# Loading a linear-attention kernel's first chunk in rows of two tokens, and working on it by pairs of batches

## The chip, the cores and the metric

The kernel runs on one core of a Trainium2 chip. The core has five engines with instruction streams of their own: TensorE (PE in the profile, its weight loads PEld), VectorE (DVE), ScalarE (ACT), GpSimd (POOL) and SyncE (SP), which here only issues transfers. Sixteen DMA engines move data. The metric is the device time of one execution in microseconds (us), as a median over runs.

## The reference

Two parts follow each other. The first is a gated linear attention with a state, for 4 batches, 8 heads, 768 tokens and a head width of 48. The second is a sum over four experts, of width 1024, weighted by normalised routing probabilities, for all 3072 tokens.

```python
f = 1.0 / (1.0 + np.exp(-f_logit))
for t in range(S):
    state = f[:, :, t, :, None] * state + np.einsum('bhd,bhe->bhde', k[:, :, t], v[:, :, t])
    y[:, :, t] = np.einsum('bhd,bhde->bhe', q[:, :, t], state)
x = y.transpose(0, 2, 1, 3).reshape(B * S, H * D)      # 3072 x 384
p = domain_probs / (domain_probs.sum(-1, keepdims=True) + 1e-09)
for e in range(E):
    h = np.maximum(x @ w1[e], 0.0)
    out += p[:, e:e + 1] * (h @ w2[e])
```

## The kernel before

The tokens are cut into 6 chunks of 128 (`C`, `T`). For each chunk `c` and batch `b`, attention is computed in its chunked form:

- `load` fetches f, k, q and v. In memory a token of one head is a row of 48 numbers, 192 bytes, and `srcs` puts the token on the partition. Chunk 0 is loaded batch by batch through SP; its v goes through POOL's queue, which casts it to bf16 on the way.
- `gate1` and `gate2` (ScalarE) compute log(1+exp(-f)). `pe_cs` (TensorE) sums it over the tokens of the chunk with the triangular matrix `Ub`, and `exps` (ScalarE) turns the sums into factors.
- `product` multiplies q and k by the factors (VectorE or POOL), `pe_tp` transposes them on TensorE, and an eviction (`ev_tp`) brings them to SBUF as `QK`.
- `pe_at` forms the scores of four head pairs, `ev_at` multiplies them by the causal mask `mask01` (VectorE), and `pe_y` multiplies the scores by v. `pe_xt` transposes the output into `xT`, the input of the experts.
- `pe_kv`, `ev_kv` and `state` bring the running state forward for the next chunk.

The experts then take all four batches of a chunk together as 512 columns: `mm_h` (L374) is the first layer, `relu` (L383, L385) evicts it, `mm_o` (L389) is the second layer and `ev_o` adds it up with the routing weight from `pn`. For chunk 0 alone, the first layer of expert 0 is cut into pieces of 256, 128, 384 and 128 columns, so that it can begin when the first two batches are ready. Attention of chunk `c+1` is spread among the experts of chunk `c`.

The order on each engine is made at build time. Every step is an `Op` with costs, a priority and dependences, and `Plan.run` is a list scheduler that places the steps on five engines ("DMA" is one of them) and hands out buffers from `rooms`. What it decides is the fixed order in which each engine then runs; the engines wait for each other through semaphores. Until the first expert matmul, the gaps that the plan shows on TensorE are filled with dummy matmuls (L644, the tile `busy`).

Transfers are queued by hand, in part. SP issues chunk 0's loads in the order of this line, in which `add_v` puts v on POOL's queue instead:

```python
for i, x in enumerate("f0 k0 q0 f1 k1 q1 f2 f3 k2 q2 v0 k3 q3 v1 v2".split()):
```

The expert weights follow on POOL's queue in eleven pieces (`w 0` to `w 10`, L246): four half pieces for the first layers of experts 0 and 1, two for the second layer of expert 0, then five whole layers. The function `after` makes some transfers wait for others: the first two v loads for k loads, the first f load of chunk 1 for weight piece 6, the last weight piece for chunk 1's k.

Of the kernel before, what the change touches and what calls it, by code (L numbers as in the profile page):

```python
# [25 lines left out]
class Plan:  # L26
# [22 lines left out]
    def take(self, o):  # L49
# [4 lines left out]
        for k in new:  # L54
            self.slot[k] = self.rooms[k[0]].pop(0)
# [47 lines left out]
def kernel(  # L103
# [35 lines left out]
             "vb": 7, "egs": 8, "QK": 4, "AT": 2, "yb": 2, "xT": 2, "h": 2, "o": 6}  # L139
# [7 lines left out]
    make_upper_triangular(nc, U, val=1.0, diag=True)  # L147
    Ub = const.tile([T, T], BF16)
    nc.gpsimd.tensor_copy(out=Ub, in_=U)
    ident = const.tile([T, T], BF16)  # L150
    make_identity(nc, ident)
# [7 lines left out]
    for i in range(rooms["e"]):  # L159
        pads["e", i] = const.tile([T, 2 * NP * P2 + HD], FP32, name=f"e{i}")  # L160
        nc.gpsimd.memset(pads["e", i][:, 0:2 * NP * P2].rearrange("t (r d i) -> t r d i", r=2, i=NP)[:, :, D:P2, :], 0.0)
    mask01 = const.tile([T, NP * T], FP32)
    nc.gpsimd.memset(mask01, 1.0)
    nc.gpsimd.affine_select(
        out=mask01, in_=mask01, compare_op=ALU.is_ge, fill=0.0,
        base=0, channel_multiplier=-1, pattern=[[0, NP], [1, T]],
    )
# [11 lines left out]
    pn = const.tile([T, E, NR], FP32)  # L179
    psm = const.tile([T, 32], FP32, name="psm")[:, 0:NR]  # L180
# [6 lines left out]
    for nm, a in (("f", f_logit), ("q", q), ("k", k), ("v", v)):  # L187
        srcs[nm] = a.rearrange("b h (c t) d -> c t (b h) d", t=T)
    ins = {}
# [7 lines left out]
        "KV": ([T, 512], FP32), "xp": ([T, KD, T], BF16), "hp": ([128, NT], FP32), "op": ([128, 512], FP32), "pp": ([T, E, NR], FP32),  # L197
    }

    def tl(kind, *key):  # L200

        if (kind, key) not in tiles:
            room = kind if kind in rooms else "ps_m" if kind in ("hp", "op", "pp") else "ps_t"
# [27 lines left out]
    def load(c, nm, b, n):  # L231
        if (c, nm) == (0, "v"):
            ins[c, nm, b] = nc.gpsimd.dma_start(out=tl("vb", c, b), in_=srcs[nm][c, :, b * H:(b + n) * H, :])  # L233
            if b < 2:
                after(ins[c, nm, b], ins[v_gate[b]])
            return
# [7 lines left out]
    def load_w(i, e, which, ks, cols):  # L244
        w, r = (w1_sb, w1_r) if which == 1 else (w2_sb, w2_r)
        ins["w", i] = nc.gpsimd.dma_start(out=w[:, e, ks, cols], in_=r[e][:, ks, cols])  # L246
        if i == w_last:
# [5 lines left out]

    def pe_pp():
        for e in range(E):
            nc.tensor.transpose(out=tl("pp")[:, e], in_=praw[:, :, e], identity=ident32)

    def probs():
        nc.vector.tensor_reduce(out=psm, in_=tl("pp").rearrange("p e r -> p r e"), axis=mybir.AxisListType.X, op=ALU.add)
# [419 lines left out]
```

## Time and profile before

| what | value |
|---|---|
| median of 3 runs | 298.34 us (298.16 to 299.37) |
| span of the profiled execution | 296.6 us |
| what lies around the span, by the median | 1.7 us |
| PE busy | 289.0 us, 97% |
| ACT / DVE / POOL busy | 59% / 43% / 36% |
| first expert matmul starts at | 19.75 us |
| dummy matmuls L644 | 34, 10.9 us busy |
| mean traffic of the DMA engines | 123 GB/s |

The profile is one execution, whose own device time is not given apart from its span; a sum that is made against the span is carried over to the median by the 1.7 us between them. A matmul's duration in the profile contains its way through the array, so the price of one in a stream is read from the distance of starts. "PE 97%" says that TensorE is occupied nearly all the time, not that it is at its peak, and the share says nothing of what a change in the head of the kernel is worth: for that the table of windows and the timeline of the first 30 us are read.

### The profile page before, as it was taken

What the parts mean: (1) busy time and instruction counts of PE and PEld (TensorE: products, weight loads), DVE (VectorE), ACT (ScalarE), POOL (GpSimd) and SP (SyncE); (2) the same over time, 40 slices, a digit from 0 to 9 for tenths busy, and PEclk for the clock granted to TensorE, in tenths of its full rate; (3) what the DMA queues carried; (4) which work ended last, traced back from release to release, by engine and by line L of the source; (5) the groups of instructions that cost most, each with busy time, mean ns of one, the idle gap of its engine ahead of it and who ended that gap; (6) DMA issues with size and microseconds to landing.
All of it is one profiled execution on the core that took longest, in us unless ns stands there. A gap on an engine that the chain in (4) does not pass through costs nothing.

```text
span 296.6 us, 5591 instructions
## 1 busy us (share of the span) xinstructions
PE 289.0 (97%) x2172; PEld 170.0 (57%) x2172; DVE 126.1 (43%) x250; ACT 174.3 (59%) x317; POOL 106.1 (36%) x180
## 2 busy tenths in 40 slices
PE   6899999999999999999999999999999999999995
PEld 2476555567777775555555555555555555555553
DVE  6786012785763673045375235243523222101223
ACT  5656656666684667777477575554475544465440
POOL 5786401138767448144449372243220000000000
PEclk9999999999999999999999999999999999999999
DMA  7999999998979999998979932102432100200002
GB/s 157 200 169 206 207 192 210 189 210 167 201 152 166 191 171 185 209 187 164 198 133 218 179 60 35 27 0 67 122 61 30 27 2 27 80 2 0 0 2 106
DMA packets 136462, 36.43 MB, mean 123 GB/s; under 512 B 126812, under 2 KB 135644, under 8 KB 136436
## 3 DMA queue, kind: packets, MB, share of 16 engines
q1 hardware_dynamic: 125188, 29.35, 52.0%
q0 software_dynamic: 11248, 6.72, 16.4%
q8 instruction: 17, 0.28, 0.4%
q14 instruction: 9, 0.07, 0.1%
HBM read 31.51 MB, written 4.72 MB: 122 GB/s over the span
## 4 chain that ended last, share of the span: by engine, by line
PE 78%; DMA 14%; POOL 3%; SPq 2%; issue 1%; ACT 1%; DVE 0%; POOLq 0%
PE ps_m L389 37%; PE ps_m L374 35%; DMA w_sb<-in_moe_w_dram 10%; DMA k<-in_k_dram 4%; SPq L237 2%; POOL w_sb L246 2%; PE ps_t L325 2%; PE ps_t L340 1%; PE ps_t L336 1%; PE ps_t L273 1%; POOL vb L233 1%; PE ps_t L346 1%; ACT e L293 1%; DVE o L396 0%; ACT xT L226 0%
## 5 line engine op out<-in xcount | busy, mean ns | idle before, releaser
L385 ACT ACTIVATE h<-ps_m 128x512 bf16<-128x512 f32 (+2 forms) x188 | 102.4, 548 | 91.9 <-PE ps_m L374 88.9
L374 PE MATMUL ps_m<-xT,w_sb 128*128 128x512 bf16 (+3 forms) x708 | 152.8, 339 | 0.6 <-ACT xT L226 0.6
L389 PE MATMUL ps_m<-w_sb,h 128*128 128x384 bf16 (+1 forms) x776 | 152.6, 324 | 0.1
L389 PEld LDWEIGHTS <-h 128*128 128x128 bf16 x776 | 75.0, 98 | 59.0 <-DMA w_sb<-in_moe_w_dram 0.3
L396 DVE SCALAR_TENSOR_TENSOR o<-ps_m,pn,o 128x384 f32<-128x384 f32 (+1 forms) x73 | 44.5, 612 | 117.3 <-PE ps_m L389 111.1
L374 PEld LDWEIGHTS <-w_sb 128*128 128x128 bf16 x708 | 65.3, 98 | 43.5 <-issue 0.7
L301 POOL TENSOR_TENSOR qk<-q,e 128x384 bf16<-128x384 f32 x18 | 21.4, 1195 | 36.5 <-ACT e L293 34.3
L360 POOL TENSOR_TENSOR Sf<-Sf,egs 48x192 f32<-48x192 f32 x40 | 20.2, 504 | 36.5 <-DVE Sf L353 34.4
L329 DVE TENSOR_TENSOR AT<-ps_t,mask 128x512 bf16<-128x512 f32 x48 | 30.2, 683 | 5.1 <-PE ps_t L325 5.1
L383 DVE TENSOR_SCALAR h<-ps_m 128x256 bf16<-128x256 f32 (+2 forms) x40 | 19.3, 499 | 26.5 <-PE ps_m L374 13.1
L293 ACT ACTIVATE e<-ps_t 128x384 f32<-128x384 f32 x48 | 26.7, 668 | 5.0 <-PE ps_t L273 3.5
L301 POOL TENSOR_TENSOR qk<-k,e 128x384 bf16<-128x384 f32 x20 | 20.2, 1013 | 8.7 <-ACT e L293 5.5
L353 DVE TENSOR_TENSOR Sf<-Sf,ps_t 48x192 f32<-48x192 f32 x40 | 14.0, 350 | 10.3 <-PE ps_t L346 9.4
L246 POOL DMA_DIRECT2D w_sb<-in_moe_w_dram x11 | 8.8, 807 | 18.5 <-DMA k<-in_k_dram 17.2
L361 POOL CAST sb<-Sf 48x192 bf16<-48x192 f32 x40 | 13.6, 340 | 2.6
L398 ACT ACTIVATE o<-ps_m,pn 128x384 f32<-128x384 f32 x22 | 12.8, 582 | 2.5 <-PE ps_m L389 1.5
L644 PE MATMUL ps_m<-busy 128*128 128x512 bf16 x34 | 10.9, 423 | 1.5 <-DVE busy L144 1.5
L265 ACT ACTIVATE ex<-f 128x768 f32<-128x768 f32 (+1 forms) x14 | 10.4, 746 | 1.8 <-DMA f<-in_f_logit_dram 1.8
L298 POOL DMA_DIRECT2D egs<-e x16 | 9.0, 563 | 6.9 <-ACT e L293 6.9
L340 PE MATMUL ps_t<-vb,AT 128*128 128x48 bf16 x192 | 11.4, 184 | 0.0
L269 ACT ACTIVATE gp<-ex 128x768 bf16<-128x768 f32 (+1 forms) x14 | 10.5, 751 | 0.3
L340 PEld LDWEIGHTS <-AT 128*128 128x128 bf16 x192 | 9.9, 97 | 1.1
(54 smaller groups left out, 120.6 us busy)
## 6 DMA issues: line engine op xcount, KB each, us to landing
out_dram<-o SPq DMA_DIRECT2D x23, 192.0 KB, 2.0
w_sb<-in_moe_w_dram POOLq DMA_DIRECT2D x5, 768.0 KB, 18.0
k<-in_k_dram SPq DMA_DIRECT2D x10, 384.0 KB, 5.6
q<-in_q_dram SPq DMA_DIRECT2D x10, 384.0 KB, 5.5
v<-in_v_dram SPq DMA_DIRECT2D x10, 384.0 KB, 5.7
f<-in_f_logit_dram SPq DMA_DIRECT2D x9, 384.0 KB, 4.6
w_sb<-in_moe_w_dram POOLq DMA_DIRECT2D x6, 384.0 KB, 9.0
f<-in_f_logit_dram SPq DMA_DIRECT2D x6, 192.0 KB, 3.8
```

The lines of the kernel that those rows point to most:

```text
L246: ins["w", i] = nc.gpsimd.dma_start(out=w[:, e, ks, cols], in_=r[e][:, ks, cols])
L293: nc.scalar.activation(out=o, in_=i, func=AF.Exp, scale=1.0 if j else -1.0)
L301: engines[eng].tensor_tensor(out=tl("qk", c, b)[:, j, :, 0:D].rearrange("t (i r) d -> t i r d", r=2), in0=tl("qk"[j], c, b // 2)[:, hh(b), ...
L329: nc.vector.tensor_tensor(out=tl("AT", c, b)[:, r].rearrange("s i t -> s (i t)"), in0=tl("A", c, b, r).rearrange("s i t -> s (i t)"), in1= ...
L340: nc.tensor.matmul(out=y[:, h * D:(h + 1) * D], lhsT=AT[:, r, i, :], rhs=vb[:, h, :], start=(c == 0), stop=True, skip_group_check=True)
L353: nc.vector.tensor_tensor(out=Sf[rows, b], in0=Sf[rows, b], in1=KV[rows, :, r, :], op=ALU.add)
L360: nc.gpsimd.tensor_tensor(out=Sf[rows, b], in0=Sf[rows, b], in1=eg, op=ALU.mult)
L374: nc.tensor.matmul(out=hp(c, e, fc, n0, n1, nf)[:, f], lhsT=w1_sb[:, e, kk, (fc + f) * 128:(fc + f + 1) * 128], rhs=tl("xT", c)[:, kk, n0: ...
L383: nc.vector.tensor_relu(out=dst, in_=src)
L385: nc.scalar.activation(out=dst, in_=src, func=AF.Relu)
L389: nc.tensor.matmul(out=tl("op", c, e, nt, part)[:, cols], lhsT=tl("h", c, e, half_of(c, nt * T))[:, fc, nt * T:(nt + 1) * T], rhs=w2_sb[:, ...
L396: nc.vector.scalar_tensor_tensor(out=o, in0=op, scalar=pe, in1=o, op0=ALU.mult, op1=ALU.add)
```

## The change

Two neighbouring tokens of one head lie side by side in memory. Chunk 0 is now read in rows of two tokens, 384 bytes, which fall on one partition. Since that leaves 64 rows for a batch, two batches share a tile of 128 partitions, alternating (`(p b)`). A unit of work is no longer one batch with 8 heads, but a pair of batches with 4 heads, both token parities `j` side by side: again 128 partitions and 384 columns.

What follows from this:

- Loads of chunk 0 move half as many rows of twice the length, in the order f0 f1 k0 k1 q0 q1 v0 v1 f2 f3 k2 k3 q2 q3, and v2 and v3 after weight piece 0. v0 waits for f1, and weight piece 1 waits for k3.
- The sums over tokens are made with two triangular matrices (`Ui` with the diagonal, `Us` without), which also keep the batches apart; four matmuls of 192 columns take the place of one of 384. The scores of a unit are 16 matmuls on 48 rows and 64 columns of the array instead of 8 on 48 rows and 128 columns. `pe_y0` has 16 matmuls on 64 rows for 8 on 128, and `pe_kv0` 32 in all for 16.
- k is copied within SBUF (`dma_kc`, eight transfers on SP's queue) into `kc`, where the batches lie in separate halves of the partitions. The eviction of the transposes (`ev_tp`) does the same sorting for q and k.
- New constants are made on VectorE at the start: `par`, `parb`, `Ui`, `Us`, `mask0`, and `mask01`, which POOL made before.
- The output tokens of chunk 0 come out sorted by parity. The routing weights are therefore transposed twice (`p_by_j`, `pe_pp`: eight transposes for four), and `store` writes chunk 0 with two transfers per tile.
- The first layers of experts 0 and 1 are computed for the first pair of batches, then for the second pair, in pieces of 256 columns. Experts 2 and 3 are as before.
- `rooms["vb"]` goes from 7 to 4. The first scores and outputs (`A0`, `y0`) take banks of `ps_m` instead of `ps_t`.

The diff, cut to its core:

```diff
-            self.slot[k] = self.rooms[k[0]].pop(0)
+            free = self.rooms[k[0]]
+            self.slot[k] = free.pop(free.index(min(free)) if k[1] in ("A0", "y0") else 0)
...
+    par = const.tile([T, 32], FP32, name="par")[:, 0:2]
+    parb = const.tile([T, 32], BF16, name="parb")[:, 0:2]
+    nc.vector.tensor_reduce(out=par, in_=ident.rearrange("t (p b) -> t b p", b=2), axis=mybir.AxisListType.X, op=ALU.add)
+    nc.vector.tensor_copy(out=parb, in_=par)
+    Ui = const.tile([T, T], BF16, name="Ui")
+    for b in range(2):
+        nc.vector.tensor_single_scalar(out=Ui.rearrange("t (p b) -> t b p", b=2)[:, b], in_=U.rearrange("t (p b) -> t b p", b=2)[:, b],
+                                       scalar=par[:, b:b + 1], op=ALU.mult)
+    Us = const.tile([T, T], BF16, name="Us")
+    nc.vector.tensor_tensor(out=Us, in0=Ui, in1=ident, op=ALU.subtract)
+    mask0 = const.tile([T, 4, P2], FP32, name="mask0")
+    for b in range(2):
+        rows = slice(b * P2, (b + 1) * P2)
+        nc.vector.tensor_copy(out=mask0[rows], in_=U[rows, rows].unsqueeze(1).broadcast_to([P2, 4, P2]))
+        nc.vector.tensor_tensor(out=mask0[rows, 2], in0=mask0[rows, 2], in1=ident[rows, rows], op=ALU.subtract)
...
-    nc.gpsimd.memset(mask01, 1.0)
...
+    nc.vector.tensor_copy(out=mask01.rearrange("s (i t) -> s i t", i=NP), in_=U.unsqueeze(1).broadcast_to([T, NP, T]))
...
+        srcs[nm, 0] = a.rearrange("b h (c p j) d -> c b p h (j d)", p=P2, j=2)[0]
...
+        if c == 0:
+            t = tl(nm, c, b // 2)[:].rearrange("(p b) (h j) d -> b p h (j d)", b=2, j=2)
+            ins[c, nm, b] = nc.sync.dma_start(out=t[b % 2], in_=srcs[nm, 0][b])
+            return
...
+        if i in w_hold:
+            after(ins["w", i], ins[w_hold[i]])
...
+        for j in range(2):
+            for jj in range(2):
+                nc.tensor.matmul(out=cs[:, j * HD // 2:(j + 1) * HD // 2], lhsT=Us if jj > j else Ui, rhs=g[:, jj * NP:(jj + 1) * NP, 0:D],
+                                 start=(jj == 0), stop=(jj == 1))
...
+    def ev_tp(c, b, js, eng):
+        o, i = tl("QK", c, b)[0:MP, js], tl("tp", c, b)[0:MP, js]
+        if c == 0:
+            o, i = o.rearrange("m q i (b p) -> m (q i) b p", b=2), i.rearrange("m q i (p b) -> m (q i) b p", b=2)
+        copy(eng, o, i)
...
+    def dma_kc(n):
+        k = tl("qk", 0, n)[:, 1].rearrange("(p b) h d -> b p (h d)", b=2)
+        for b in range(2):
+            nc.sync.dma_start(out=kc[n // 2][b * P2:(b + 1) * P2, n % 2].rearrange("p h d -> p (h d)"), in_=k[b])
...
+    def pe_at0(n):
...
+                        rows, tok = slice(r * P2, r * P2 + D), slice(b * P2, (b + 1) * P2)
+                        nc.tensor.matmul(out=a_of(0, n, r)[tok, 2 * i + j, :].rearrange("s (k t) -> s k t", k=2),
+                                         lhsT=QK[rows, 1, 2 * j + i, tok], rhs=Q[rows, i, :, tok], start=True, stop=True)
...
+    def pe_y0(n):
...
+                        nc.tensor.matmul(out=y_of(2 * g + b)[:, h * D:(h + 1) * D], lhsT=AT[tok, r, 2 * i + j, :], rhs=v0[g][tok, h, j, :],
+                                         start=(j == 0), stop=(j == 1), skip_group_check=True)
...
-    v_gate, issued = [(0, "k", 1), (0, "k", 2)], []
+    v_gate, w_hold, issued = {0: (0, "f", 1)}, {1: (0, "k", 3)}, []
...
-    for i, x in enumerate("f0 k0 q0 f1 k1 q1 f2 f3 k2 q2 v0 k3 q3 v1 v2".split()):
+    for i, x in enumerate("f0 f1 k0 k1 q0 q1 v0 v1 f2 f3 k2 k3 q2 q3".split()):
...
-            for fcs, n0, n1, xs, nf in ((range(0, KF // 2), 0, N2, LO, 1), (range(0, KF // 2, 2), N2, NT - T, [2], 2),
-                                        (range(KF // 2, KF), 0, NT - T, LO + [2], 1), (range(0, KF, 4), NT - T, NT, [3], 4)):
-                zip_units([(c, 0, fc, n0, n1, xs, nf) for fc in fcs], [])
-            unit[0] = u0 + 2 * KF
+            for e, n0, xs in ((0, 0, LO), (1, 0, LO), (0, N2, HI)):
+                zip_units([(c, e, fc, n0, n0 + N2, xs) for fc in range(KF)], [], 0.5)
+            zip_units([(c, 1, fc, N2, NT, HI) for fc in range(KF)], ol(c, 0, ALL))
+            unit[0] = u0 + 3 * KF
```

A new planner function `attention0` takes the place of `attention` for chunk 0. It adds, for each unit n (0 and 1 for batches 0 and 1, 2 and 3 for batches 2 and 3), gates, sums, factors, products, transposes, scores, masks and y in this order of priority, with the priorities of the second pair behind those of the first; k comes ahead of q, and each is transposed and evicted by itself. Products of units 0 and 1 are for VectorE alone, of units 2 and 3 for VectorE or POOL.

## The prediction

> **What bounds the kernel now.** The page first. TensorE is busy almost throughout, and the DMA engines are saturated for the first fifth only:
>
> ```profile
> PE 289.0 (97%) x2172; PEld 170.0 (57%) x2172; DVE 126.1 (43%) x250; ACT 174.3 (59%) x317; POOL 106.1 (36%) x180
> PE   6899999999999999999999999999999999999995
> DMA  7999999998979999998979932102432100200002
> ```
>
> A table of windows then says where TensorE's idle time lies (columns: stretch, length, busy of PE, weight loads, DVE, ACT, POOL, clock, DMA share, GB/s):
>
> ```profile
> 0.00:19.50 19.50, 16.01 (x151) 8.15 (x152) 13.98 (x34) 11.95 (x27) 14.41 (x29) 1.00 1.22 171
> 19.50:24.00 4.50, 4.50 (x51) 3.55 (x50) 3.26 (x11) 3.35 (x10) 2.49 (x3) 1.00 1.25 206
> 24.00:28.20 4.20, 4.20 (x53) 3.02 (x51) 3.58 (x11) 2.68 (x5) 2.52 (x6) 1.00 1.30 205
> 28.20:59.20 31.00, 30.89 (x186) 16.84 (x184) 8.90 (x15) 19.10 (x34) 6.28 (x13) 1.00 1.18 200
> ```
>
> Before 19.5 most of PE's 16 us are the dummy matmuls (34 of them, 10.9 us). From 19.75, the first expert matmul, PE has no hole to speak of. So the end is the time of that matmul (call it D), plus all PE work still left at D, plus stalls. The timeline of PE around it:
>
> ```profile
> 19.75 0.82 PE L374 MATMUL ps_m<-xT,w_sb 128*128 128x256 bf16 x6
> 20.41 0.33 PE L365 MATMUL ps_t<-ident,yb 128*128 128x128 bf16 x3
> 20.57 0.82 PE L374 MATMUL ps_m<-xT,w_sb 128*128 128x256 bf16 x6
> 21.23 0.36 PE L340 MATMUL ps_t<-vb,AT 128*128 128x48 bf16 x8
> ...
> 22.59 0.33 PE L365 MATMUL ps_t<-ident,yb 128*128 128x128 bf16 x3
> ...
> 24.22 0.84 PE L346 MATMUL ps_t<-vb,qk 128*128 128x96 bf16 x16
> 24.90 3.44 PE L374 MATMUL ps_m<-xT,w_sb 128*128 128x128 bf16 x33
> ```
>
> Starts, not durations, give the price, because a duration holds about 0.16 of pipeline. Six 256-column matmuls take 20.41-19.75 = 0.66, 0.11 each. The x33 group (24 of 128 columns, 9 of 512) lasts from 24.90 to 28.18: at 0.216 for 512 columns the short ones cost 0.055 each. All shapes stream at one rate per column, so regrouping the first expert layers earns nothing by itself. Of chunk 0's attention only 0.16+0.20+0.17+0.68 = 1.2 us lies after D; the rest ran where PE was idle.
>
> The chain of waits up to 60 us is transfers:
>
> ```profile
> 20.53 21.10 DMA w_sb<-in_moe_w_dram
> 42.07 7.75 DMA k<-in_k_dram
> 50.37 8.82 DMA w_sb<-in_moe_w_dram
> 59.24 0.82 PE ps_m L389 x4
> ```
>
> The last weights land at 59.19 and are used at 59.24: PE and DMA are in step. A change must bring both forward.
>
> **What the Trainium skill says.** "DMA: Bandwidth & Descriptors", section "Why small descriptors are slow (HBM only)", gives about 3 cycles per packet beside 32-byte beats; "How a descriptor splits into AXI transactions" says a read starts at a 256-byte boundary, lost bytes paid. Rows of 192 bytes at steps of 192 then cost 6, 12, 10 and 8 beats, mean 9, plus 3: 12 cycles. Rows of 384 cost 12 and 16, mean 14, plus 3: 17. The trace agrees on the first: from the issue-to-landing times, first-chunk loads land about 0.95 us apart (f1 6.24, k2 11.05, five loads between), 64 rows per engine, 14.7 ns a row, against 14.1 at the page's 850 MHz fabric clock. A 384-byte load is not in the trace. Estimate: 0.94 x (512 x 17)/(1024 x 12) = 0.66. Bounds 0.50 (half the rows at the old price) and 0.94 (bytes decide). "TensorEngine Tiling (Array Packing)", section "Key Properties", says tiles run in parallel but changing the mode drains the array. This trace shows eight 48-row products in 0.33 us (60.64 to 60.97), i.e. two side by side, and shows no four-quadrant use.
>
> **Loads.** Sixteen first-chunk loads save 0.28 each: 4.5 us. Added: eight SBUF copies of k, 64 rows of 1 KB each. No such copy is in the trace; by bytes at the 210 GB/s of the early windows 0.3 each, 2.5 in all, and 1.2 at twice that rate; they sit on SP's queue behind the f load of chunk 1, hence after weight piece 6. KV sums wait for them, but are needed only by y of chunk 1 (61 us), 25 us later: no cost there. Weight pieces 1 to 5, now landing at 22.0, 24.1, 26.0, 28.0, 29.9, come 4.5 earlier; the last at 59.2-4.5+(1.2 to 2.5) = about 56.5. Piece 1 gets a new wait, on the last k. Behind it on POOL stand only weight issues (seven took 5.51 us), states, and products that VectorE can take; before it 12.4 us of transfers are queued, so the DMA engines don't run dry.
>
> **When D comes.** A unit is now two batches by half the heads, the same 384 columns; two units finish the first pair. First bytes at 2.0 as now; f1 at 2.0+1.32+0.57 (f0's excess) = 3.9, against f0 alone at 3.5. ScalarE: both units' gates, 4 x 0.52, to 6.15; exps 0.43 each, first k product possible at 6.7. VectorE is not free: its setup ended at 5.45 and gains ten small constant operations. None is in the trace; by like rows (0.10 for a cast, 0.18 for a tensor-scalar, 0.25 for a reduce) 1.8, bounds 1.2 and 2.5: 7.2. Then its line is the path: four products x 0.56, one eviction 0.4, four mask products x 0.64 = 5.2, plus 0.5 for the one place where it waits on TensorE: 12.9. The end of the chain: y 0.5, its copy 0.55, transposes 0.34, copy 0.48, hops and weight load 0.6: D = 15.4. Credit 19.75-15.4 = 4.35. v, gated on f1, lands near 9 to 10 (now 12.8 and 15.65) and isn't late; q3 lands near 15.
>
> **PE work left at D.** The second pair (units 2, 3) now runs inside the dense part. Their cumulative sums and k transposes fit before D (k3 lands near 12.4). After D: q transposes 8 x 0.055 = 0.44; scores 16 per unit, 0.33 (four at once) to 0.66 (two), take 0.5: 1.0; y 16 per unit at 0.025: 0.8; output transposes 0.33; KV 32 instead of 16 half-height matmuls, 0.68 to 1.36, take 1.0; routing transposes, now eight and behind the first pair, 0.127 each: 1.0. Sum 4.6, minus the 1.2 of now: debit 3.4 (bounds 2.3 and 4.5).
>
> **Stalls.** Weights: piece 1 at 17.5; four units of 0.33 and the routing bring PE there at 17.7. Piece 3 at 21.5 against 22.5. Narrow, but enough. The second pair: VectorE's products 2.24, masks 2.56, copies about 1.5 end near 20, its output tiles near 22; PE's first-pair work for two experts (5.3) plus what is mixed in reaches 23.7. 16 relus at 0.39 on ScalarE alone fill 6.2 of those 8. PE's order is fixed, so an attention instruction whose eviction is late holds the expert matmuls behind it: I put 0.6, bounds 0 and 3. The doubled stores of chunk 0 (four more SP issues at about 0.4) the copy that sorts the routing weights by parity (24 rows of 512, at most 0.6 by the 512-column mask product), and fewer v buffers (4 for 7) lie beside work with slack: nothing.
>
> **Sum.** 296.6 - 4.35 + 3.4 + 0.6 = 296.25. The median of the runs is 1.7 above that profile's span; 298.34 - 0.35 = **298.0**, no change. About 0.5% (1.5 us) is what can be told from none: 296.8 to 299.8. The earlier start is real, but bought with attention work that was free in the idle head and now isn't.
>
> **Rivals.** *Cheap quadrants*: scores, y and KV overlap fully (debit 2.3), setup is 1.2, D = 14.8 (credit 4.95), no stall: 295.7. For it: before D PE is slack, and 48-row pairs overlap already. Against: VectorE's 5.2 us line. Chance 0.24.
> *In-order stalls* (slower): attention of the second pair is chained VectorE to PE at ten hand-overs; late by 0.35 each, PE loses about 3: 298.34-0.95+3 = 300.4. It decides once the hand-overs fall behind by more than 0.25 on average, since ten of those eat the 0.95 and 1.5 besides. For it: POOL is issuing weights and VectorE must take all products. Against: ScalarE and VectorE kept up between 19.5 and 28.2 now, where PE had no hole, though with three hand-overs only. Chance 0.24.
> *The rows don't get cheaper* (0.94 per load): weight piece 3 stays at 26.0, PE holds at expert 1's second half; then 1.3+5.2 of expert work and 1.0 of KV end at 33.5, where now 31.4 stands for the same work: 300.4. For it: the DMA engines are full already. Against: the row price fits the page. Chance 0.08.
> The forecast: 0.44, its own range 296.9 to 299.5. Over all cases 295.7 to 300.9. Faster 0.24, same 0.44, slower 0.32.
>
> **What would show it.** Right: first expert matmul near 15.4; first-chunk loads landing 0.6 to 0.7 apart; PE without holes from 15.4 to 28 but with score, y and KV groups between expert matmuls; last weights near 56.5. Wrong: D before 14.5, PE idle of over 1.5 us between D and 30 with VectorE or weights as releaser, or 0.9 per load.

## Result, and the profile after

The changed kernel takes 306.52 us (median of 4 runs, 305.5 to 307.14) against 298.28 for the kernel before beside it: ratio 1.026, 95% interval 1.022 to 1.030. Forecast were 298.0 us and no change, with a range to 300.9. The profiled execution has a span of 304.6 us, 8.0 more than before, with 1.8 around it (before: 1.7).

The page of the changed kernel, the lines that answer to those of before, and the granted clock:

```profile
PE 294.1 (97%) x2265; PEld 176.4 (58%) x2265; DVE 137.4 (45%) x275; ACT 170.7 (56%) x316; POOL 104.4 (34%) x178
PE   5969999999999999999999999999999999999995
PEclk9975999999999999999999999999999999999999
DMA  6999999992899987999796943001432100100002
```

TensorE is again full from the fourth slice on (a slice is 7.6 us), and it is emptier in the first and third than before. Its granted clock falls in the third and fourth. Windows of the same run (stretch, length, busy of PE, weight loads, DVE, ACT, POOL, clock, DMA share, GB/s):

```profile
0.00:20.00 20.00, 13.37 (x138) 7.72 (x139) 14.64 (x40) 10.88 (x25) 9.87 (x23) 0.98 1.02 181
20.00:40.00 20.00, 19.78 (x194) 14.71 (x195) 10.44 (x24) 9.16 (x23) 5.10 (x7) 0.76 1.17 189
```

The second stretch has hardly an idle moment, but a mean clock of 0.76. The first expert matmul, D in the prediction, starts at 23.40. It was at 19.75 before and was forecast for 15.4. What follows D takes 304.6 - 23.4 = 281.2, where it took 276.85: 4.35 more, forecast 3.4 + 0.6 = 4.0. Two sums must be kept apart. The forecast span was 296.25, and of the miss of 8.35 against it **8.0 us lie in D**. Against the kernel before, the span grew by about as much, but D is only 3.65 later; the other 4.35 lie behind D.

VectorE's timeline up to the first pair's masks (start, duration, engine, line, operation; in brackets the idle time before it and what ended it):

```profile
7.71 0.54 DVE L349 TENSOR_TENSOR qk<-k,e 128x384 bf16<-128x384 f32 x1
...
10.49 0.69 DVE L247 COPY QK<-ps_t 112x512 bf16<-112x512 bf16 x1 [1.07 <-PE ps_t L362]
...
11.56 0.69 DVE L247 COPY QK<-ps_t 112x512 bf16<-112x512 bf16 x1
12.92 0.69 DVE L247 COPY QK<-ps_t 112x512 bf16<-112x512 bf16 x1 [0.67 <-PE ps_t L362]
13.53 1.28 DVE L430 TENSOR_TENSOR AT<-ps_m,mask 128x512 bf16<-128x512 f32 x2
14.72 1.28 DVE L430 TENSOR_TENSOR AT<-ps_t,mask 128x512 bf16<-128x512 f32 x2
18.05 1.83 DVE L349 TENSOR_TENSOR qk<-q,e 128x384 bf16<-128x384 f32 x2 [2.05 <-DMA q<-in_q_dram]
19.80 0.55 DVE L247 CAST yb<-ps_m 128x384 bf16<-128x384 f32 x1
```

The masks are done at 16.0 (forecast 12.9), and then VectorE waits 2.05 us for the second pair's q. A copy of the first pair's output (`yb`) stands behind these q products until 19.80, though its y is done at 18.6. TensorE in the same stretch, and POOL below:

```profile
14.67 0.54 PE L409 MATMUL ps_m<-v,AT 64*128 64x48 bf16 x16
17.49 0.40 PE L362 MATMUL ps_t<-ident,qk 128*128 128x128 bf16 x4 [2.27 <-POOL qk L349]
17.72 0.59 PE L811 MATMUL ps_m<-busy 128*128 128x512 bf16 x2
18.25 0.37 PE L409 MATMUL ps_m<-v,AT 64*128 64x48 bf16 x16
...
19.94 1.03 PE L362 MATMUL ps_t<-ident,qk 128*128 128x128 bf16 x8 [0.66 <-DVE qk L349]
20.77 0.85 PE L470 MATMUL ps_t<-ident,yb 128*128 128x128 bf16 x6
21.41 1.06 PE L811 MATMUL ps_m<-busy 128*128 128x512 bf16 x2
22.40 1.07 PE L394 MATMUL ps_t<-QK 48*64 48x128 bf16 x32
23.40 1.46 PE L479 MATMUL ps_m<-xT,w_sb 128*128 128x256 bf16 x6
```

```profile
7.61 1.42 POOL L253 DMA_DIRECT2D v<-in_v_dram  x2
15.64 0.76 POOL L270 DMA_DIRECT2D w_sb<-in_moe_w_dram  x1 [6.61 <-DMA k<-in_k_dram]
16.42 1.01 POOL L349 TENSOR_TENSOR qk<-k,e 128x384 bf16<-128x384 f32 x1
```

Read them together. The second y of the first pair (18.25) could have run at 16.0. Ahead of it in TensorE's fixed order stand the k transposes of the second pair (17.49). They wait for POOL's product (16.42), which needs the last k chunk of the second pair and besides stands behind a weight issue of 0.76 that was held for the same chunk. That chunk landed at 15.36, the last q at 17.93. In the kernel before, with its dearer rows, they had landed at 14.40 and 15.35: there three of the four v loads and all weights were issued from 11.35 on, while the changed kernel issues all four v loads and a weight piece between 5.3 and 9.0, beside the second pair's loads.

In the same way the output transposes L470 stand behind the second pair's q transposes, and the expert matmul behind the second pair's scores. The last six matmuls take 1.46 us, where before D's six took 0.82: half rate.

### The profile page after: what moved, and what is told of

The parts are those of the page before. It is cut to its first block, busy times and chain, and to the rows that moved or that the text cites. A ratio compares the mean times of both kernels' runs of the same rounds, so it can differ in the third digit from the quotient of the medians.

```text
span 304.6 us, 5812 instructions
## 1 busy us (share of the span) xinstructions
PE 294.1 (97%) x2265; PEld 176.4 (58%) x2265; DVE 137.4 (45%) x275; ACT 170.7 (56%) x316; POOL 104.4 (34%) x178
## 4 chain that ended last, share of the span: by engine, by line
PE 87%; DMA 5%; SPq 5%; DVE 2%; ACT 1%; issue 0%; DVEq 0%
PE ps_m L479 39%; PE ps_m L494 39%; DMA q<-in_q_dram 3%; SPq L259 2%; DMA f<-in_f_logit_dram 2%; PE ps_t L425 2%; SPq L261 1%; PE ps_t L445 1%; PE ps_t L441 1%; PE ps_t L311 1%; PE ps_t L451 1%; PE ps_t L362 1%; DVE qk L349 1%; SPq L377 1%; PE ps_t L470 0%
## 5 line engine op out<-in xcount | busy, mean ns | idle before, releaser
L479 PE MATMUL ps_m<-xT,w_sb 128*128 128x512 bf16 (+1 forms) x720 | 155.6, 340 | 0.2 <-DVE pn L296 0.2
L490 ACT ACTIVATE h<-ps_m 128x512 bf16<-128x512 f32 (+1 forms) x188 | 99.6, 532 | 98.4 <-PE ps_m L479 96.1
L479 PEld LDWEIGHTS <-w_sb 128*128 128x128 bf16 x720 | 68.7, 99 | 42.4 <-issue 0.6
L488 DVE TENSOR_SCALAR h<-ps_m 128x256 bf16<-128x256 f32 (+1 forms) x52 | 25.0, 490 | 23.6 <-PE ps_m L479 21.1
L434 DVE TENSOR_TENSOR AT<-ps_t,mask 128x512 bf16<-128x512 f32 x40 | 24.9, 683 | 4.8 <-PE ps_t L425 4.8
L247 POOL CAST vb<-v 128x384 bf16<-128x384 f32 x16 | 7.9, 507 | 34.7 <-issue 15.9
L353 POOL TENSOR_TENSOR qk<-k,e 128x384 bf16<-128x384 f32 x18 | 17.9, 998 | 4.5 <-DMA k<-in_k_dram 3.1
L811 PE MATMUL ps_m<-busy 128*128 128x512 bf16 x19 | 8.9, 561 | 1.5 <-DVE busy L145 1.5
L445 PE MATMUL ps_t<-vb,AT 128*128 128x48 bf16 x160 | 10.0, 185 | 0.0
```

The costliest lines, as they stand in the source:

```text
L353: engines[eng].tensor_tensor(out=tl("qk", c, b)[:, j, :, 0:D].rearrange("t (i r) d -> t i r d", r=2), in0=tl("qk"[j], c, b // 2)[:, hh(b), ...
L434: nc.vector.tensor_tensor(out=tl("AT", c, b)[:, r].rearrange("s i t -> s (i t)"), in0=tl("A", c, b, r).rearrange("s i t -> s (i t)"), in1= ...
L445: nc.tensor.matmul(out=y[:, h * D:(h + 1) * D], lhsT=AT[:, r, i, :], rhs=vb[:, h, :], start=(c == 0), stop=True, skip_group_check=True)
L479: nc.tensor.matmul(out=hp(c, e, fc, n0, n1, nf)[:, f], lhsT=w1_sb[:, e, kk, (fc + f) * 128:(fc + f + 1) * 128], rhs=tl("xT", c)[:, kk, n0: ...
L488: nc.vector.tensor_relu(out=dst, in_=src)
L490: nc.scalar.activation(out=dst, in_=src, func=AF.Relu)
```

## Experiments

**The theory after the result (A):** the first pair's masks are ready at 16.0 and D comes 7.4 later because the fixed orders put work of the second pair, whose loads are late, ahead of it; undo that and most of the 8 us return. **Rivals (B):** the rows did not become cheap; TensorE's half rate is the cause; the regrouped expert layers cost time; or it is the extra attention work behind D. Ratios are against the kernel before, run beside each. D, spans and waits are those of one profiled execution each.

**1. Regrouped expert layers alone.** The kernel before, with only its first expert layers cut by pairs of batches:

```diff
...
+            for e, n0, xs in ((0, 0, LO), (1, 0, LO), (0, N2, HI)):
+                zip_units([(c, e, fc, n0, n0 + N2, xs) for fc in range(KF)], [], 0.5)
+            zip_units([(c, 1, fc, N2, NT, HI) for fc in range(KF)], ol(c, 0, ALL))
...
```

> Kernel before with one part of the change alone: first layers of experts 0 and 1 by pairs of batches in pieces of 256 columns, loads and attention as before. Theory A (the regrouping earns and costs nothing by itself): 298.0 to 298.8 us. Theory B (it needs weight pieces 2 and 3 earlier and waits for them, or ScalarE and VectorE can't evict pieces of 256 fast enough): 299.5 to 301 us.

298.48 us, ratio 1.000 (0.999 to 1.001). In this kernel the regrouping costs and earns nothing, as the prediction had it. The loss belongs to the loads and the attention of chunk 0, or to what the regrouping does only together with them.

**2. First weight piece behind the second pair's k.**

```diff
-    v_gate, w_hold, issued = {0: (0, "f", 1)}, {1: (0, "k", 3)}, []
+    v_gate, w_hold, issued = {0: (0, "f", 1)}, {0: (0, "k", 3)}, []
```

> Changed kernel, but weight piece 0 (and v2, v3 behind it on POOL's queue) waits for k3, and piece 1 no longer does. The orders of TensorE and VectorE up to the first expert matmul stay as they are. Theory A (the second pair's loads are late because v and weight piece 0 share the DMA engines with them, and TensorE's fixed order stands still behind k3): k3 lands near 12 instead of 15.4, TensorE's wait for the k product shrinks from 2.3 us to under 0.5, the first expert matmul comes at 19 to 20 instead of 23.4, the clock stays full, 300 to 301 us. Theory B (the loads are limited by their own rows or by SP's issue, not by the sharing): k3 at 14 or later, 304 to 306 us, and weights later besides.

(The edit also lifts the wait of weight piece 1, and v2 and v3 follow behind piece 0.) 306.2 us, ratio 1.025 (1.023 to 1.027). The last k landed at 13.11 instead of 15.36, but D moved only to 22.79, less than single profiles differ (experiment 10). TensorE now stood 2.47 us waiting for the second pair's gates at 13.12, ahead of the first pair's last transposes in its order, and the granted clock from 12 to 20 was 0.57. An earlier k alone doesn't help as long as the fixed order takes the second pair first. Theory A (300 to 301) missed; B had the whole right (304 to 306), but for a k at 14 or later.

**3. The order alone.**

```diff
-deps=[km], takes=[pt_("tp")]
+deps=[km] + (N[1:2] if n >= 2 else []), takes=[pt_("tp")]
...
-deps=[eq, ld[0, "q", 2 * g], ld[0, "q", 2 * g + 1]]
+deps=[eq, ld[0, "q", 2 * g], ld[0, "q", 2 * g + 1]] + (EY[:2] if n >= 2 else [])
```

The second pair's k transposes now stand behind the first pair's y, its q products behind the first pair's output copies.

> Changed kernel with the planned order alone altered: the second pair's transposes of k come behind y of unit 1 on TensorE, and its q products behind the output copies of the first pair on VectorE. No transfer changes. Theory A (in-order stalls: work of the first pair stands behind work that waits for k3 and q3): first expert matmul near 18 instead of 23.4, 301 to 302 us, then limited by weight pieces 1 to 3, which land near 20.7, 23.3 and 26.5. Theory B (late weights set the end of this stage anyway): the first matmul is earlier, the end is not, 305 to 307 us.

D fell to 20.30, 3.1 earlier: the order was that much of the miss. (Experiment 4, with the same order, has 20.30 again.) Yet the kernel took 310.28 us, ratio 1.038 (1.035 to 1.042): expected were 301 to 302 or 305 to 307, and it is slower than both. TensorE's timeline of this kernel shows where the gain went:

```profile
42.69 0.65 PE L494 MATMUL ps_m<-w_sb,h 128*128 128x384 bf16 x3
46.92 0.21 PE L417 MATMUL ps_t<-v,kc 64*128 64x96 bf16 x1 [3.59 <-DMA kc<-qk]
47.41 0.34 PE L417 MATMUL ps_t<-v,kc 64*128 64x96 bf16 x7 [0.28 <-DMA kc<-qk]
48.07 0.89 PE L417 MATMUL ps_t<-v,kc 64*128 64x96 bf16 x8 [0.32 <-DMA kc<-qk]
```

These waits are 4.2 us, and for some 3 us after them TensorE ran at half rate. The plan put the KV sums ahead of where the copies of k (`dma_kc`) land. In the changed kernel those copies occupied SP's queue from 35.05 for 11.9 us too, and KV ran at 49.25 and 54.34 without a wait, because the plan happened to have it later.

**4. The order, and the k copies right behind the loads.**

```diff
-on(dma_kc, n), -453 + n, deps=[km, wd[2, 1][0]],
+on(dma_kc, n), -980 + n, deps=[km],
```

> The planned order of e2_order, and the eight copies of k queued on SP right behind q3 instead of behind chunk 1's first f load. Theory A (e2_order repaired the head, and lost it again because KV sums stood waiting for the copies of k, 4.2 us, and for what followed from it): the wait of the KV matmuls for the copies is gone, first expert matmul near 20, 302 to 304 us. Theory B (the loss in e2_order is not in that wait; another takes its place): 307 us or more.

303.68 us, ratio 1.016 (1.013 to 1.019), span 301.3, as expected (302 to 304). KV runs at 27.55 and 29.41 with no wait. Order and copies together return 3.3 of the 8.0 us of span, 2.8 by the medians.

**5. More of the order.** To the kernel of 4: the second pair's gates behind the first pair's evictions, its k products behind the first pair's output copies, its k transposes behind the first pair's output transposes.

```diff
-deps=[ld[0, "f", 2 * g], ld[0, "f", 2 * g + 1]]
+deps=[ld[0, "f", 2 * g], ld[0, "f", 2 * g + 1]] + (ET if n >= 2 else [])
...
-deps=[ek, ld[0, "k", 2 * g], ld[0, "k", 2 * g + 1]]
+deps=[ek, ld[0, "k", 2 * g], ld[0, "k", 2 * g + 1]] + (EY[:2] if n >= 2 else [])
...
-deps=[km] + (N[1:2] if n >= 2 else [])
+deps=[km] + (XT[:2] if n >= 2 else [])
```

> As e6_order_kc, and all steps of the second pair stand behind those of the first on every engine: gates behind the first pair's evictions on ScalarE, products behind its output copies, k transposes behind its output transposes. Theory A (the first pair is held up by what stands ahead of it in the fixed orders and waits for f3, k3 and q3): nothing of the first pair waits for a load of the second; first expert matmul at 17 to 18, 300 to 302 us. Theory B (the first pair's own chain is that long): 20 or later, 303 us or more.

308.44 us, ratio 1.031 (1.027 to 1.035), in theory B's range (303 or more), though not for its reason. D came at 19.12, before B's 20, but after three matmuls TensorE was idle for 0.55 and 1.36 us, and the next expert matmuls ran at half rate: POOL's last k product now stood behind six weight issues (16.33 to 20.85). Putting one queue in order made another late.

**6. The second pair's loads: what they cost alone.** v left out of the head (issued only behind the last q, and with it all weights, which follow on POOL's queue):

```diff
-    v_gate, w_hold, issued = {0: (0, "f", 1)}, {1: (0, "k", 3)}, []
+    v_gate, w_hold, issued = {0: (0, "q", 3)}, {}, []
...
-    for i, x in enumerate("f0 f1 k0 k1 q0 q1 v0 v1 f2 f3 k2 k3 q2 q3".split()):
+    for i, x in enumerate("f0 f1 k0 k1 q0 q1 f2 f3 k2 k3 q2 q3 v0 v1".split()):
```

> Changed kernel in which every transfer of POOL's queue (v and all weights) waits for q3, so that the twelve loads of two-token rows run alone. A measurement of the price of a load. Theory A (rows of 384 bytes cost 0.66 as predicted, and the sharing made them late): the last q lands near 10.6, eleven loads of 0.66 after the first. Theory B (a load costs about 0.77, as the 255 GB/s between 3 and 8 us of the changed kernel say, because bytes count nearly as much as rows): near 12. Theory C (0.9 and more, no gain from longer rows): 13.5 or later. The whole time is of no interest; it is over 306 us, since v and the weights come late.

(One execution, 308.88 us.) The window of the loads in this kernel:

```profile
3.00:11.00 8.00, 6.31 (x38) 3.74 (x37) 6.57 (x19) 5.05 (x13) 0.00 (x0) 1.00 1.01 262
```

Twelve loads landed from 3.92 to 12.36: 8.44/11 = 0.77 each, not 0.66 and not 0.94. The last k landed at 10.82 and the last q at 12.36, where in the changed kernel, beside four v loads and one weight piece, it was 15.36 and 17.93. Sharing cost the second pair 4.5 to 5.6 us. That fits the bytes: four v loads and the piece are 1.18 MB, 4.5 us at the 262 GB/s of this window. The row price accounts for less: 11 loads at 0.77 instead of 0.66 are 1.2 us.

**7. Row length.** Each of these loads cut into two transfers of 192-byte rows:

```diff
-            ins[c, nm, b] = nc.sync.dma_start(out=t[b % 2], in_=srcs[nm, 0][b])
+            for j in range(2):
+                ins[c, nm, b] = nc.sync.dma_start(out=t[b % 2][:, :, j * D:(j + 1) * D], in_=srcs[nm, 0][b][:, :, j * D:(j + 1) * D])
```

> Changed kernel with each first-chunk load of f, q and k cut into two transfers by token parity, i.e. rows of 192 bytes again, in the same layout, order and plan. Theory A (the longer rows do save transfer time, if less than predicted): loads land later by 0.1 to 0.2 us each, the last q 2 us later, 307.5 to 309 us. Theory B (the row length saves nothing): 306 to 307 us, landing times as in the changed kernel.

312.36 us, ratio 1.045 (1.042 to 1.049), D 28.64: more than either theory said. SyncE's own lines tell why this doesn't measure the row:

```profile
0.73 2.83 SPq L260 DMA_DIRECT2D f<-in_f_logit_dram  x4
3.60 2.67 SPq L260 DMA_DIRECT2D k<-in_k_dram  x4
6.32 2.67 SPq L260 DMA_DIRECT2D q<-in_q_dram  x4
```

An issue of 512 rows takes 0.67 us on SP, for 192 bytes a row as for 384 (0.66 there). Two issues for a load make 1.34, so SP sets the pace, and the traffic from 4 to 14 us is 163 GB/s. It decides nothing on the price of a row, but it shows that SP's pace in the changed kernel, 0.68 a load, was already about the forecast 0.66; a load of 0.50, the prediction's lower bound, SP could not have issued.

**8. Half rate behind D.** Dummies in TensorE's waits ahead of the second pair's transposes:

```diff
+        o.pad += {"tpk 0.2": 9, "tpq 0.2": 2}.get(o.name, 0)
```

> Changed kernel with eleven more dummy matmuls (nine ahead of unit 2's k transposes, two ahead of its q transposes), which run while TensorE would stand waiting there. Theory A (part of the loss is TensorE's clock, which fell to 0.5 from 19.4 to 28.7 us after those waits): clock 1.00 throughout, 3 to 4 us saved, 302.5 to 303.5 us. Theory B (the clock record has no part in the time, or other holes bring it down just the same): 306 to 307 us.

305.62 us, ratio 1.023 (1.021 to 1.025). In this profile, the slowest of its four executions, the low clock stood earlier, from about 13.3 to 18.6; most of the added dummies began only at 17.94, so they didn't put it there. D fell back to 25.50, and what follows D ran at a clock of 1.00 to 40 us and took 279.7 instead of 281.2. The same instructions, from D to the group behind the second y, in the changed kernel and here:

```profile
23.40 1.46 PE L479 MATMUL ps_m<-xT,w_sb 128*128 128x256 bf16 x6
29.50 1.16 PE L479 MATMUL ps_m<-xT,w_sb 128*128 128x256 bf16 x9
```

```profile
25.50 0.83 PE L479 MATMUL ps_m<-xT,w_sb 128*128 128x256 bf16 x6
29.46 0.72 PE L479 MATMUL ps_m<-xT,w_sb 128*128 128x256 bf16 x5
```

That is 6.10 against 3.96: behind D the half rate costs the changed kernel 2.1 us. (Of these, 0.5 went again here, as KV waited for the copies of k at 49.8.) Expected 302.5 to 303.5: missed, as the dummies delay D.

**9. Order, copies, the first weight piece held, k products on VectorE.** To the kernel of 4, besides the held weight piece of 2: the second pair's k products on VectorE alone and behind the first pair's masks, its k transposes behind the first pair's output transposes.

```diff
-            pe = {"DVE": 0.5} if n < 2 else {"DVE": 0.5, "POOL": 1.2}
+            pe = {"DVE": 0.5}
...
-deps=[ek, ld[0, "k", 2 * g], ld[0, "k", 2 * g + 1]]
+deps=[ek, ld[0, "k", 2 * g], ld[0, "k", 2 * g + 1]] + (EA[:4] if n >= 2 else [])
...
-deps=[km] + (N[1:2] if n >= 2 else [])
+deps=[km] + (XT[:2] if n >= 2 else [])
```

> The reordered kernel with early key copies, in which besides: the first weight piece (and so everything behind it on POOL's queue) is issued only once the last k chunk of the second pair has landed, the k products of the second pair are VectorE's alone and stand behind the first pair's masks, and the second pair's key transposes stand behind the first pair's x transposes. Theory A (what is left of D's lateness is the second pair's loads sharing the DMA engines with v and the first weight piece, and POOL's product behind its weight issue): the last k chunk lands near 13.4 instead of 15.4 to 15.9, D, the first expert matmul, falls from 20.3 to between 18.3 and 19.0, and the whole to 301 to 302.5. Theory B (the first pair's own chain, at half clock and behind the gates, is what bounds once the order is mended): D within 0.5 of 20.3, the whole 303 to 304.5.

303.34 us, ratio 1.0145 (1.011 to 1.019); the last k landed at 12.95, D 19.15, span 301.5. D is a little later than theory A expected (18.3 to 19.0), and the whole lies in the range of theory B (303 to 304.5): of the 1.15 us by which D came earlier than in experiment 4, nothing that can be told from scatter reaches the end. TensorE's timeline has it again further on:

```profile
79.12 0.40 PE L425 MATMUL ps_t<-QK 48*128 48x128 bf16 x8 [1.23 <-DMA QK<-qk]
89.39 0.48 PE L311 MATMUL ps_t<-gp,Ub 128*128 128x384 bf16 x2 [0.82 <-ACT gp L306]
```

These are waits for the transposing transfers and the gates of a later chunk; the second had been 0.46 in experiment 4, the first 0.33.

**10. The same with five dummies ahead of the first cumulative sum.** The edit stood ahead of the loop that sets all counts of dummies, which overwrote it:

```diff
+    for o in done:
+        o.pad += {"cs 0.0": 5}.get(o.name, 0)
     for o in done:
         if o.engine == "PE" and o.start <= first:
             o.pad, t = int((o.start - t) / (0.42 if t < 7.0 else 0.25)), o.end
```

So the dummies are missing, and this is the program of 9 once more. It tests neither theory, but shows the scatter.

> The kernel with the first weight piece held and the second pair's k products on VectorE, and five more dummy matmuls of 512 columns ahead of TensorE's first cumulative sum, in the 2 us for which TensorE waits for the first gates. Theory A (that idle stretch is what puts TensorE at half rate from 6.3 to 11.5, where four 128-column transposes took 0.63 instead of 0.40, and the first pair's chain is bound by it): the four transposes take 0.40, the first pair's masks are done 0.6 to 1.0 earlier and D and the whole fall by as much against the kernel without these dummies. Theory B (VectorE and the loads set the first pair's masks, TensorE's rate does not): D and the whole stay within 0.3.

304.35 us, ratio 1.017 (1.011 to 1.022), D 21.01 instead of 19.15, and 281.9 behind D instead of 282.35. Of D no difference under 2 us between single profiles should be read, and of the whole none under 1 us.

**11. Four dummies there, placed after that loop.**

```diff
+    for o in done:
+        o.pad += {"cs 0.0": 4}.get(o.name, 0)
```

> The kernel with the first weight piece held and the second pair's k products on VectorE, with four more dummy matmuls of 512 columns ahead of TensorE's first cumulative sum, where TensorE waits 1.9 us for the first gates. Theory A (that wait puts TensorE at half rate for some of the stretch from 6 to 11.5, where four 128-column transposes take 0.63 instead of 0.40, and the first pair's chain is bound by it): the four transposes take 0.40, the first pair's masks are done 0.6 to 1.0 earlier than in the kernel without these dummies, D falls by as much, and the whole by 0.6 to 1.2. Theory B (the loads and VectorE set the first pair's masks): D and the whole stay within the 1 us by which runs of one kernel differ here.

304.01 us, ratio 1.019 (1.016 to 1.022), D 20.05. TensorE in this kernel:

```profile
8.30 0.40 PE L362 MATMUL ps_t<-ident,qk 128*128 128x128 bf16 x4
...
12.41 0.24 PE L315 MATMUL ps_t<-gp,Ui 128*128 128x192 bf16 x1 [2.56 <-ACT gp L306]
```

The transposes run at full rate (0.40; without the dummies 0.63), and TensorE then waits 2.56 us for the second pair's gates instead of 1.2. The masks start at 13.87, against 13.93. Theory B holds: with late loads the half rate is hidden.

**12. v behind the second pair's gates** (to the kernel of 9):

```diff
-{0: (0, "f", 1)}, {0: (0, "k", 3)}
+{0: (0, "f", 3)}, {0: (0, "k", 3)}
...
-"f0 f1 k0 k1 q0 q1 v0 v1 f2 f3 k2 k3 q2 q3"
+"f0 f1 k0 k1 q0 q1 f2 f3 v0 v1 k2 k3 q2 q3"
```

> The kernel with the first weight piece held and the second pair's k products on VectorE, in which besides the first two v chunks are issued only when the second pair's gates (f) have landed, where they had been issued after the first pair's; eight dummy matmuls ahead of the first y are left out to keep TensorE's queue as short. Theory A (v takes the DMA engines' turns from f, k and q of the second pair, as it and the first weight piece did in the changed kernel): the second pair's f lands near 9.6 instead of 11.3 to 12.2, the last k near 11 instead of 13.2 to 13.8, TensorE's wait for the second pair's gates (1.2 to 2.3 us before the cumulative sum of the third unit) goes, the first pair's masks are done 1 to 1.5 earlier, and D falls from 19.2 to 21.0 to between 17.8 and 19.0, the whole to 301 to 302.5. Theory B (v is only moved in time: the first y then waits for v0 and v1, which land after 15.5): D 19.5 to 21, the whole 303 to 305.

D came at 18.48, before the old kernel's 19.75; the second pair's f landed at 9.38. But the whole took 303.95 us, ratio 1.018 (1.014 to 1.022): behind D there were 285.3 us (this profile is the slowest of the four executions, 305.6), with waits of TensorE for gates and transposing transfers of later chunks (0.74 at 70.9, 1.22 at 78.7, 0.70 at 106.0, 1.03 at 118.5). Eight dummies ahead of the first y were left out. D is as theory A had it, the whole as theory B.

**13. Both, early loads and full rate.** The four dummies of 11 in the kernel of 12.

> The kernel with v moved behind the second pair's gates, with four more dummy matmuls of 512 columns ahead of TensorE's first cumulative sum (that kernel had D, the first expert matmul, at 18.48, its first pair's masks done at 15.7, and the first sixteen 128-column transposes at 0.63 for four; the prediction had D at 15.4). Theory A (TensorE's half rate between 6 and 11.5 costs the first pair nothing only where it waits for the second pair's loads afterwards anyway; with those loads early it is on the path): the transposes take 0.40, VectorE's first copy of a transpose starts at 9.2 instead of 10.4, the first pair's masks are done by 14.3 to 14.9, D falls to between 17.0 and 17.8. Theory B (TensorE idles as much, and the half rate comes back between 12 and 18): masks at 15.3 or later, D 18.2 to 19. Either way the whole stays between 302.5 and 304.5, as the third chunk's loads hold TensorE later on.

304.12 us, ratio 1.017 (1.016 to 1.019), D 19.01. The first pair's masks start at 12.81 instead of 13.25, 0.44 earlier; then y waits 0.91 for v (landed 15.77). D has the number of theory B (18.2 to 19), but not for its reason: the half rate did not come back (the dummies at 16.3 took 0.22 a step, and the clock from 6 to 19 was 1.00); v, issued later, now held y. The chain of waits of this kernel (start, length, what) shows what now sets the rest:

```profile
11.86 7.10 DMA w_sb<-in_moe_w_dram
19.25 1.78 POOL w_sb L270 x2
21.02 21.93 DMA w_sb<-in_moe_w_dram
42.97 5.60 DMA f<-in_f_logit_dram
```

The ninth weight piece (`w 8`), issued at 21.02, lands at 42.95. In the chain of before it was issued at 20.53 and landed at 41.63. The transfers have gained nothing by then.

What each D was followed by. The last column sums TensorE's waits behind D that its timeline marks (0.16 us and longer):

| kernel | D | behind D | span | waits behind D |
|---|---|---|---|---|
| before | 19.75 | 276.85 | 296.6 | 0.57 |
| changed | 23.40 | 281.2 | 304.6 | 0.39, and 2.1 of half rate |
| 2, weight piece held | 22.79 | 281.8 | 304.6 | 2.67 |
| 3, order | 20.30 | 287.5 | 307.8 | 6.02, and half rate at 48 to 51 |
| 4, order and copies | 20.30 | 281.0 | 301.3 | 1.41 |
| 5, more order | 19.12 | 287.2 | 306.3 | 4.13, and half rate at 22 to 29 |
| 7, rows of 192 | 28.64 | 281.1 | 309.7 | 1.74 |
| 8, dummies behind | 25.50 | 279.7 | 305.2 | 0.89 |
| 9 and its repeat | 19.15, 21.01 | 282.35, 281.9 | 301.5, 302.9 | 2.47, 2.42 |
| 11, dummies ahead | 20.05 | 281.55 | 301.6 | 1.87 |
| 12, v later | 18.48 | 285.3 | 303.8 | 4.12 |
| 13, both | 19.01 | 283.6 | 302.6 | 3.25 |

No profile comes below 301.3, and no median below 303.34. When D comes before 20, the time behind it grows.

What is left when waits and half rate are taken off is work: 276.3 before; 278.7 to 279.3 in the changed kernel and in 2, 7 and 8, which keep its order; 279.5 to 281.2 in 4 and 9 to 13, where the second pair's scores stand behind D. (3 and 5 are left out, as their half rate was not measured.) The 8.0 us of the changed kernel are thus 3.65 in D, 2.4 of work, 2.1 of half rate and 0.2 less of waits.

So theory A is right about D, but not about the 8 us. Of the 4.7 that experiment 4, at full rate, still loses to the kernel before, 0.55 are in D, 0.8 in waits, and 3.3 are work behind D, the last of the rivals (B). No experiment took that work away; it is found by subtraction. The groups that can be read in experiment 4 (scores 0.57, y 0.62, output transposes 0.33, KV 0.90, routing transposes 1.06) sum to 3.5, less the 1.2 of before 2.3. Where the last 1.0 is spent stays open.

## Why the prediction was wrong, step by step

**D = 15.4, the start of the first expert matmul, is the step that failed**; it was 23.40. Its two halves failed separately.

*Masks at 12.9, measured 16.0.* Setup ended at 7.78 for 7.2 (additions 2.3, inside the bounds). Four products and four mask products took what was said. But "one eviction 0.4" was three on VectorE at 0.69 each: 1.7 more. And "0.5 for the one place where it waits on TensorE" was 1.07 + 0.67, 1.2 more. The sum, 3.5, is about the 3.1 seen. f1 landed near 5.0, not 3.9, but VectorE's setup hid most of that.

*From masks to D 2.5, measured 7.4.* The sum was of durations of the first pair's own steps; it put what stands between them in the queues at nothing, without a reason. The order was fixed by a plan that counted on the second pair's k ahead of the first pair's y, and in truth the last k landed at 15.36. Changing only the order took 3.1 off (experiment 3). In experiment 9 the masks were done at 16.4 and D came 2.75 later: there the forecast of 2.5 holds. In its repeat it was 3.5 from 17.55, partly at half rate.

**The load price.** The estimate of 0.66 came from the Trainium skill, "DMA: Bandwidth & Descriptors", sections "Why small descriptors are slow (HBM only)" and "How a descriptor splits into AXI transactions". Alone the loads took 0.77, so the measurement decides against the estimate's full gain, and SP's issue pace of 0.68 stands just below it. The larger error was "k3 near 12.4, q3 near 15": the loads came at 15.36 and 17.93, some 3.0 later each, of which the row price explains at most 1.2. Without v and the weights beside them they came at 10.82 and 12.36 (experiment 6), so that most of their lateness is sharing. With the order mended, holding the weights and moving v behind the second pair's gates brought D to 18.48 (experiment 12).

**"Weight pieces 1 to 5 come 4.5 earlier": no.** They landed at 20.76, 23.30, 26.57, 28.55 and 30.47, where before they landed at 21.98, 23.95, 25.84, 27.74 and 29.75: the first two 1.2 and 0.65 earlier, the others 0.7 to 0.8 later. The last weights, forecast near 56.5, came at 66.97 (before 59.19). Experiment 13, with D at 19.01, has them at 22.74 to 31.08 and 60.26. In the first 20 us the DMA engines moved 172 GB/s before and 189 to 191 in experiments 12 and 13: 20 x 18 = 0.36 MB more, 1.8 us at 200 GB/s. The eight copies of k move 8 x 64 KB = 0.52 MB, 2.6 us at that rate, and in these two runs four of them lie inside the 20 us. What the longer rows give, the copies take. This arithmetic and the landings agree; no run took the copies away altogether, so the split isn't shown by itself. It suggests, though no run shows it, that even a D of 15.4 would not have ended the kernel at 296.

The prediction's account of transfers stopped at 60 us. It called the DMA engines saturated for the first fifth only, but its own DMA line stands at 7 tenths or more up to the 23rd slice, 170 us. The waits of experiments 9, 12 and 13 lie in that stretch, at 70 to 120.

**Behind D: the sum came out, its parts did not.** 3.4 + 0.6 was forecast and 4.35 measured, which is in part luck. The 3.4 held 1.44 for the second pair's q transposes and scores; in the changed kernel these ran ahead of D (19.94 and 22.40). What stood behind D was 2.4 of work, and 2.1 of half rate that the prediction didn't have; stalls were 0.2 less than before. Where the order is the one that the prediction supposed (experiment 4), the work is 3.3 more than before, and there 3.4 was right. "KV: no cost" was right in the changed kernel only because its plan was late; with an earlier D the same copies cost 4.2 us (experiment 3). "Regrouping earns nothing by itself" was right (experiment 1).

**The rivals.** "In-order stalls" had the right mechanism in the wrong place, and was priced at 300.4: it looked for late hand-overs behind D, between VectorE and TensorE. They were ahead of D, between pairs, and came from transfers. "Cheap quadrants" was right on the scores: 32 of them took 0.57 to 0.78 us (experiments 4 and 13), 0.28 to 0.39 a unit where 0.5 was taken, and y took 0.31 a unit for 0.4; but D made that count for little. "The rows don't get cheaper" is answered by experiment 6: 0.77, not 0.94. None of the three signs named as "wrong" showed itself (D before 14.5, holes behind D, 0.9 per load when they run alone): a late D was not among them. Every unknown cost had been bounded, but the start of the path had 15.4 and, in one rival, 14.8, and nothing on the late side.

## To carry to other kernels

When a change splits work into a first and a second part to start earlier, price the first part by what stands ahead of each of its instructions in every queue, with the second part's loads at landing times that count every byte issued beside them. An order written by a plan is right only as long as its landing times are: here loads for later work that came late held the head up by 5 us (7.4 instead of 2.5). And where transfers and TensorE are in step, count the bytes that a change adds (here copies for a new layout) against the ones it makes cheaper, before crediting an earlier start.

## What the runs showed of the hardware that was not expected

- In the changed kernel TensorE ran at half rate, by the distances of starts, between 6 and 11.5 us (four 128-column transposes 0.63 us instead of 0.40, each group followed by a dummy at 0.43 a step instead of 0.22) while the granted clock of the windows from 3 to 17 us stood at 1.00. In two profiles of one program (9 and 10) the first cumulative sum at 6.1 took 0.32 and 0.24. The Trainium skill, "TensorE: Matmul & The Clock Gate", Part 1, says that the window which decides on half rate runs freely, so that the same kernel meets it at another place in each run; these two profiles fit that.
- An issue on SP was no cheaper for half the bytes: 0.67 us for 512 rows of 192 bytes, 0.66 for 512 rows of 384.
- Where the half rate falls could not be steered with dummies. The same four ahead of the first sum were followed by half rate from 14.4 to 17.7 in experiment 11 (clock 0.57 from 14 to 18), and by none up to 19 in experiment 13; and without them the transposes of experiment 2 ran at full rate too (0.40 from 9.57 on).
- Sixteen score matmuls on 48 rows and 64 columns of the array took 0.28 us (32 from 21.05 to 21.62, experiment 4); eight on 48 rows and 128 columns took 0.33 in the kernel before (60.64 to 60.97).
